# Two decode attention blocks on one core: the last four heads of an output projection in 2 KB rows, and the first output stored ahead

## The chip, the cores and the metric

The kernel runs on one core of one Trainium2 chip. The metric is the device time of one execution in microseconds (us), lower is better. Before the change the median of three runs is 665.49 us (665.38 to 665.52).

## The reference

Two independent attention blocks, A and B, of the same sizes, each for a single query token against a cache of 8192 positions and 32 heads of 128. Their outputs of 512 numbers stand side by side in the result.

```python
def _A_ref(x, k_cache, v_cache, wq, wo):          # _B_ref computes the same (rep is 1)
    B, Sq, D = x.shape                             # 1, 1, 512
    H, Dh = 32, 128
    q = (x @ wq).reshape(B, Sq, H, Dh).transpose(0, 2, 1, 3)
    scores = jnp.einsum("bhqd,bhkd->bhqk", q, k_cache) * (Dh ** -0.5)
    p = _softmax(scores, axis=-1)
    o = jnp.einsum("bhqk,bhkd->bhqd", p, v_cache)
    return o.transpose(0, 2, 1, 3).reshape(B, Sq, H * Dh) @ wo     # wo: 4096 x 512
...
return jnp.concatenate([a, b], axis=-1)            # (1, 1, 1024), bf16
```

## The kernel before

**Loops and groups.** The work is 16 groups of four heads: eight groups of A, then eight of B. A group's K and V are 8 MB each; K goes to one of two slots of `kn`, V to the only slot `vn`. In each of the 16 rounds VectorE multiplies K by the query (L279), TensorE sums over the head dimension with identity matmuls into the two tiles of `rps` (L424, L430), VectorE reduces them to scores `s_sb` (L307), ScalarE takes exponentials (L379), and TensorE multiplies by V into `acc` (L483). One round later VectorE turns `acc` into the group's four output columns: `part()` (L284, L287, L291), a small matmul `total_of_group()` (L436), and `outs()` (L296).

**The order of transfers.** One queue, SyncE's, issues nearly everything in the order in which it is written: K and V by turns, then `wo` of A (4 MB), the last V, and `wo` of B in the six pieces of the table `WOB` (L89): heads 0 to 15, 16 to 23, 24 to 27, 28 and 29, 30, 31. The flag in the table says how a piece lies in memory. With True, partition p takes n consecutive rows of `wo` of the n heads, one run of n KB. With False, partition p takes row p of each head, runs of 1 KB.

**What the layout costs.** With the runs of n KB, a head's output vector no longer fits the rows that its `wo` tile holds, so the outputs of these heads are redistributed first: `spread(i)` (VectorE, L328) writes them into `zb` under a mask, a matmul with `jsel` (L449) moves them into PSUM, and `lay(i)` (VectorE, L336) copies them to `o2`. This is done for A (32 heads) and for the three long pieces of B in the last round, in `mid()` on TensorE and after the loop on VectorE. The last four heads, whose outputs come last, are written to `o2` directly (L347).

**The end of the program.** On TensorE, after the last matmuls with V: 16 matmuls with the first piece of B (`partial`, L443) into `yps[0]`, which also holds A's sum over its 32 heads; five matmuls whose result nobody reads (`turn_over(5)`, L461); `total_of_group()` for the last four heads; four fp32 passes with `sel16` (L496) that add up the rows of `yps[0]` into `yps[1]`, after ScalarE has copied them to `yc` (L382; `yc` is a view of `qmem` and shows under that name); and 32 matmuls for B's heads 16 to 31 (L505), each half of a head's 512 columns, a row for A and a row for B each. Before each piece of `wo` TensorE waits for its semaphore. Then ScalarE and VectorE each cast half of the columns to `out_sb` (L384, L349), and SyncE stores both outputs with one DMA of two 1 KB rows (L232).

Of the kernel before, what the change touches and what calls it, by code (L numbers as in the profile page):

```python
# [8 lines left out]
BF16 = mybir.dt.bfloat16  # L9
F32 = mybir.dt.float32  # L10

P = 128
# [33 lines left out]
def bass_concat_heads__mha_block_cached__gqa_block_cached__decode_kernel(  # L46
# [26 lines left out]
    G = 4  # L73
    HP = P // G
# [3 lines left out]
    N = NA * GA  # L78
# [7 lines left out]
    NG = T // W  # L86


    WOB = [(0, 16, True), (16, 8, True), (24, 4, True), (28, 2, False), (30, 1, False), (31, 1, False)]  # L89
    RG = [32, 16, 8, 4]  # L90
    NH = NOUT // 2

    with ExitStack() as st:
# [11 lines left out]
        WO = H * NOUT  # L105
# [3 lines left out]
        yc = qmem[:, 0:NOUT]  # L109
# [21 lines left out]
        o2 = sb("o2", [P, NA * H, NA], BF16)  # L131
        mask = {g: sb("mask%d" % g, [P, P // g], BF16) for g in RG}
        jsel = {g: sb("jsel%d" % g, [P, g], BF16) for g in RG}
        out_sb = sb("out_sb", [NA, NOUT], BF16)

        def ps(name, shape):
            return ec(nc.psum_tensor(name, shape, F32))
# [2 lines left out]
        acc = ps("acc", [P, 512])  # L140
# [2 lines left out]
        misc = ps("misc", [P, 512])  # L143
        yps = [ps("yps%d" % i, [P, 512]) for i in range(2)]
        EX = 128
        lay_ps = [misc, yps[1], acc, mtp]

        def sem(name):
            return ec(nc.semaphore(name))
# [3 lines left out]
        s_wob = [sem("s_wob%d" % g) for g in range(len(WOB))]  # L153
        s_k = [sem("s_k%d" % i) for i in range(2)]

        c_pool, c_sel, c_mul, c_sr, c_g, c_gm, c_self, c_st, c_o, c_rl, c_yd = (
            sem(n) for n in ("c_pool", "c_sel", "c_mul", "c_sr", "c_g", "c_gm", "c_self", "c_st", "c_o", "c_rl", "c_yd"))

        c_qa, c_nb, c_p, c_ya = (sem(n) for n in ("c_qa", "c_nb", "c_p", "c_ya"))

# [25 lines left out]
        @block.sync  # L186
        def _(e):
            load_wq(e, 0)
            for a in range(NA):
                e.dma_start(xrow[a:a + 1, :], xs[a][0]).then_inc(s_x, 16)  # L190

            def group(x, n):
                a, i = divmod(n, GA)
                return x[a][0, G * i:G * (i + 1)].rearrange("h (p t) d -> (h p) (t d)", p=HP)

            def load_k(n):
                if n >= 2:
                    e.wait_ge(c_red, RED * (n - 1))
                e.dma_start(kn[:, n % 2 * KS:(n % 2 + 1) * KS], group(ks, n)).then_inc(s_k[n % 2], 16)

            def load_v(n):
                if n:
                    e.wait_ge(c_pv, n + 1)
                else:
                    e.wait_ge(c_q, N)
                e.dma_start(vn[:], group(vs, n)).then_inc(s_v, 16)

            def load_wob(g):
                h0, n, rows = WOB[g]
                src = wos[1][h0 * Dh:(h0 + n) * Dh, :]  # L210
                dst = kn[:, WO + h0 * NOUT:WO + (h0 + n) * NOUT]
                if rows:
                    src = src.rearrange("(p j) n -> p (j n)", p=P)
                elif n > 1:
                    src = src.rearrange("(j p) n -> p j n", p=P)
                    dst = dst.rearrange("p (j n) -> p j n", j=n)
                e.dma_start(dst, src).then_inc(s_wob[g], 16)

            load_k(0)
            load_k(1)  # L220
            for n in range(N - 1):
                load_v(n)
                if n + 2 < N:
                    load_k(n + 2)
            e.wait_ge(c_red, RED * (N - 1))
            e.dma_start(kn[:, 0:WO], wos[0].rearrange("(p j) n -> p (j n)", p=P)).then_inc(s_woa, 16)
            load_v(N - 1)
            for g in range(len(WOB)):
                load_wob(g)
            e.wait_ge(c_yd, 1)  # L230
            e.wait_ge(c_ya, 2)
            e.dma_start(out[0].rearrange("o (a n) -> (o a) n", a=NA), out_sb[:]).then_inc(s_out, 16)  # L232
            e.wait_ge(s_out, 16)

        def once(e):

# [6 lines left out]
        def _(e):  # L243
            with once(e):
# [48 lines left out]
                def outs(dst):  # L293
                    w_self()
                    w_ex()
                    e.tensor_tensor(dst, mtp[:, EX:EX + G], rinv[:], ALU.mult).then_inc(c_o, 1)  # L296
# [20 lines left out]
                        outs(oD[:, bass.ds(r * G, G)])  # L317


                todo = [(0, 0, H)] + [(1, h0, n) for h0, n, rows in WOB if rows]  # L320
                e.wait_ge(c_o, N)

                def spread(i):
# [15 lines left out]

                spread(0)  # L340
                spread(1)
                for i in range(len(todo)):
                    lay(i)
                    if i + 2 < len(todo):
                        spread(i + 2)
                part()
                outs(o2[:, NA * H - G:NA * H, NA - 1])  # L347
                e.wait_ge(c_y, 2)
                e.tensor_copy(out_sb[:, 0:NH], yps[1][0:NA, 0:NH]).then_inc(c_yd, 1)  # L349


        @block.scalar
        def _(e):
            load_wq(e, 1)
            with once(e):
                w_q = _Stepped(e, c_q, 1, 1)
                w_bc = _Stepped(e, c_bc, 1, 1)
                w_nb = _Stepped(e, c_nb, 1, 1)
                w_pv = _Stepped(e, c_pv, 1, 1)
                e.wait_ge(c_pv, 1)  # L360
                e.copy(xT[:].rearrange("p (a c) -> p c a", c=C),
                       misc[:, 0:C * NA].rearrange("p (c a) -> p c a", a=NA)).then_inc(c_qa, 2)
                with e.Fori(0, N // 2) as r:
                    for j in range(2):
                        w_q()
                        for h in range(G):
                            p = slice(h * HP, (h + 1) * HP)
                            i = e.copy(qflat[p, bass.ds(r * (2 * Dh) + j * Dh, Dh)],  # L368
                                       yps[j][p, h * Dh:(h + 1) * Dh])
                        i.then_inc(c_qa, 1)  # L370
                e.wait_ge(c_pool, NPOOL)
                with e.Fori(0, N):
                    w_bc()
                    e.activation(negb[:], bmp[:, 0:G], AF.Copy, scale=-scale).then_inc(c_nb, 1)  # L374
# [7 lines left out]
                e.copy(yc, yps[0][:]).then_inc(c_ya, 1)  # L382
                e.wait_ge(c_y, 2)
                e.copy(out_sb[:, NH:NOUT], yps[1][HP:HP + NA, 0:NH]).then_inc(c_ya, 1)  # L384


        @block.tensor
        def _(e):
            with once(e):
# [51 lines left out]
                def partial(h):  # L441
                    k = h % G * HP
                    return e.matmul(yps[0][k:k + NA, :], o2[:, h, :], wo_rows(h), start=False, stop=False,  # L443
                                    skip_group_check=True)

                def mid():
                    for i, (a, h0, n) in enumerate([(0, 0, H)] + [(1, h0, n) for h0, n, rows in WOB if rows]):
                        e.wait_ge(c_rl, (1, 2, 4, 6)[i])
                        e.matmul(lay_ps[i][:, 0:n], zb[:, i % 2, :], jsel[n][:], start=True,  # L449
                                 stop=True).then_inc(c_rm, 1)  # L450
                    e.matmul(yps[0][:], zrow[:], ones_bf[0:1, 0:1].broadcast_to([1, 512]), start=True,
                             stop=False, skip_group_check=True)
                    e.wait_ge(c_rl, 8)
                    e.wait_ge(s_woa, 16)
                    for h in range(H):
                        partial(h)

                def turn_over(n):

                    with e.Fori(0, n):  # L460
                        e.matmul(rps[:, 0, :], ident[:], kn[:, 0:512], start=True, stop=True)  # L461
# [27 lines left out]
                for h in range(H, H + WOB[0][1]):  # L489
                    m = partial(h)  # L490
                m.then_inc(c_y, 1)
                turn_over(5)
                total_of_group()
                e.wait_ge(c_ya, 1)
                for b in range(2):
                    e.matmul(yps[1][b * HP:b * HP + NA, 0:NH], sel16[:, 0, 0:NA],  # L496
                             yc[:, b * NH:(b + 1) * NH], start=True, stop=False, skip_group_check=True)
                for g in range(1, len(WOB)):
                    h0, n, rows = WOB[g]
                    e.wait_ge(s_wob[g], 16)  # L500
                    for h in range(h0, h0 + n):
                        for b in range(2):
                            if h == H - G - 1 and b:
                                e.wait_ge(c_o, N + 1)
                            m = e.matmul(yps[1][b * HP:b * HP + NA, 0:NH], o2[:, H + h, :],  # L505
                                         wo_rows(H + h)[:, b * NH:(b + 1) * NH], start=False,
                                         stop=(h == H - 1), skip_group_check=True)
                m.then_inc(c_y, 1)
# [28 lines left out]
```

## Time and profile before

| what | value |
|---|---|
| median of 3 runs | 665.49 us (665.38 to 665.52) |
| profiled execution: its span, first to last instruction | 663.5 us |
| PE, DVE, ACT busy | 58%, 55%, 12% of the span |
| DMA engines | nine tenths busy or more in nearly every slice, 430 GB/s mean |
| mean granted TensorE clock | 0.79 |

The profiled execution has no time of its own beside its span; 2.0 us lie between the span and the median. PE is TensorE's matmul, PEld its weight load, DVE is VectorE, ACT ScalarE, SP SyncE; a number after L is a line of the kernel. In the views by time the first column is the start in us from the span's start, the second the duration. A matmul's duration includes its pipeline, so a stream of matmuls is read by the distance of their starts. The tile names leave the buffer's number out: `yps` is `yps[0]` or `yps[1]`, `o` is `o2`, `sel` is `sel16`, `m` is `m1`.

### The profile page before, as it was taken

Reading aid. Unit: us, or ns where it says so; the run is one execution under the profiler, and the core shown is the slowest. Engines: PE = TensorE matmul, PEld = TensorE weight load, DVE = VectorE, ACT = ScalarE, POOL = GpSimd, SP = SyncE. Lnnn points to the kernel's source line nnn. Section 1 sums busy time; section 2 is a strip of 40 time slices with the busy share of each in tenths; the row PEclk is TensorE's granted clock in tenths of the full one; section 3 lists DMA queues with packets and bytes.
Section 4 is the critical chain, followed back from the end, with each engine's and each line's share of the span. In section 5 each row is a group of like instructions: output and inputs, shape, how many; then the busy total and the mean of one; then the engine's idle time right before and its main releaser. Section 6 shows DMA issues by size and latency. Waiting matters only on the chain.

```text
span 663.5 us, 7942 instructions
## 1 busy us (share of the span) xinstructions
PE 385.8 (58%) x2402; PEld 191.8 (29%) x2402; DVE 362.5 (55%) x249; ACT 76.6 (12%) x212; POOL 2.3 (0%) x12
## 2 busy tenths in 40 slices
PE   0455685854819185481918548191854819185488
PEld 0122232423315042330404233140423314032233
DVE  1009494848292754829274482927548292744821
ACT  0370202020010202001020200102020010202002
POOL 1000000000000000000000000000000000000000
PEclk9995988786959678695967869596786959678697
DMA  9999998999999999999999999999999999999997
GB/s 379 443 442 442 442 442 379 442 442 442 442 442 442 391 431 442 442 442 442 442 399 423 442 442 442 442 442 411 411 442 442 442 442 442 415 407 442 440 444 317
DMA packets 6041, 285.23 MB, mean 430 GB/s; under 512 B 660, under 2 KB 1176, under 8 KB 1304
## 3 DMA queue, kind: packets, MB, share of 16 engines
q1 hardware_dynamic: 5896, 281.03, 98.0%
q10 hardware_dynamic: 144, 4.19, 1.5%
q14 instruction: 1, 0.01, 0.0%
HBM read 285.21 MB, written 0.00 MB: 430 GB/s over the span
## 4 chain that ended last, share of the span: by engine, by line
DMA 72%; PE 22%; DVE 2%; issue 2%; ACT 1%; ACTq 0%; DVEq 0%; SPq 0%
DMA vn<-in_B_v_cache_dram 34%; DMA vn<-in_A_v_cache_dram 34%; PE acc L483 14%; PE rps L430 5%; DMA xrow<-in_B_x_dram 3%; PE yps L413 2%; DVE kn L279 1%; ACT qmem L368 1%; PE yps L443 1%; ACT pt L379 0%; PE yps L505 0%; DVE s_sb L307 0%; PE rps L461 0%; PE misc L478 0%; PE rps L424 0%
## 5 line engine op out<-in xcount | busy, mean ns | idle before, releaser
L279 DVE TENSOR_TENSOR kn<-kn,qmem 128x16384 bf16<-128x16384 bf16 x32 | 276.7, 8688 | 55.2 <-ACT qmem L368 43.0
L430 PE MATMUL rps<-kn,ident 128*128 x1024 | 236.8, 383 | 0.4
L483 PE MATMUL acc<-vn,pt 128*32 128x512 bf16 x1024 | 92.3, 531 | 145.7 <-DMA vn<-in_B_v_cache_dram 75.3
L307 DVE TENSOR_REDUCE s_sb<-rps 128x64 f32<-128x512 f32 x64 | 44.1, 691 | 165.1 <-PE rps L430 165.1
L430 PEld LDWEIGHTS rps<-kn,ident 128*128 128x128 bf16 x1024 | 96.4, 98 | 111.0 <-issue 22.6
L483 PEld LDWEIGHTS acc<-vn,pt 128*32 128x32 bf16 x1024 | 60.3, 127 | 171.1 <-issue 155.9
L374 ACT ACTIVATE negb<-bmp 128x4 f32<-128x4 f32 x16 | 2.8, 173 | 539.7 <-PE bmp L472 539.7
L379 ACT ACTIVATE pt<-s_sb,negb 32x256 bf16<-32x256 f32 x64 | 54.9, 858 | 4.3 <-ACT negb L374 2.9
L478 PE MATMUL misc<-rsum,ones_f 128*128 128x4 f32 x32 | 9.4, 365 | 56.4 <-ACT pt L379 56.4
L284 DVE TENSOR_SCALAR om<-acc,msk 128x128 f32<-128x128 f32 x16 | 5.6, 350 | 42.8 <-PE acc L483 42.8
L478 PEld LDWEIGHTS misc<-rsum,ones_f 128*128 128x128 f32 x32 | 8.0, 312 | 58.6 <-ACT pt L379 57.8
L413 PE MATMUL yps<-vn,xT 128*128 x64 | 17.3, 419 | 6.2 <-ACT qmem L368 4.2
L287 DVE SCALAR_TENSOR_TENSOR om<-acc,msk,om 128x128 f32<-128x128 f32 x48 | 16.8, 351 | 5.9
L470 PE MATMUL mtp<-ident_f,m 128*1 128x128 f32 x32 | 6.1, 270 | 22.6 <-DVE m L312 22.6
L424 PE MATMUL rps<-ones_bf,zrow 1*128 1x1 bf16 x64 | 11.0, 171 | 13.4 <-DVE kn L279 10.8
L424 PEld LDWEIGHTS rps<-ones_bf,zrow 1*128 1x128 bf16 x64 | 5.8, 91 | 40.6 <-issue 40.6
L368 ACT CAST qmem<-yps 32x128 f32 x64 | 16.4, 256 | 7.0 <-PE yps L413 6.3
L379 ACT ACTIVATION_READ_ACCUMULATOR pt<-s_sb,negb 32x1 f32 x64 | 15.9, 249 | 0.0
L399 PE MATMUL misc<-ident,xrow 2*128 2x2 bf16 x4 | 0.3, 166 | 22.8 <-DMA xrow<-in_B_x_dram 22.8
L413 PEld LDWEIGHTS yps<-vn,xT 128*128 x64 | 6.6, 103 | 16.5 <-issue 13.7
L472 PE MATMUL bmp<-gm,ones_f 1*128 1x4 f32 x32 | 6.1, 258 | 7.3 <-DVE gm L314 7.3
L470 PEld LDWEIGHTS mtp<-ident_f,m 128*1 128x1 f32 x32 | 1.4, 80 | 30.5 <-DVE m L312 30.5
(58 smaller groups left out, 57.0 us busy)
## 6 DMA issues: line engine op xcount, KB each, us to landing
vn<-in_B_wq_dram ACTq DMA_DIRECT2D x1, 4096.0 KB, 21.9
vn<-in_A_wq_dram SPq DMA_DIRECT2D x1, 4096.0 KB, 21.7
kn<-in_A_wo_dram SPq DMA_DIRECT2D x1, 4096.0 KB, 27.4
kn<-in_B_wo_dram SPq DMA_DIRECT2D x1, 2048.0 KB, 27.7
kn<-in_B_wo_dram SPq DMA_DIRECT2D x1, 1024.0 KB, 29.7
kn<-in_B_wo_dram SPq DMA_DIRECT2D x1, 512.0 KB, 30.5
kn<-in_B_wo_dram SPq DMA_DIRECT2D x1, 256.0 KB, 30.8
kn<-in_B_wo_dram SPq DMA_DIRECT2D x2, 128.0 KB, 30.6
```

Of the source, the lines that this page charges most:

```text
L279: e.tensor_tensor(k, k, qflat[:, bass.ds(q, Dh)].unsqueeze(1).broadcast_to([P, HM, Dh]), ALU.mult).then_inc(c_mul, 2)
L287: e.scalar_tensor_tensor(om[t % 2][:], acc[:, t * Dh:(t + 1) * Dh], msk[:, t:t + 1], om[(t + 1) % 2][:], ALU.mult, ALU.add).then_inc(*((c_ ...
L307: e.tensor_reduce(s_sb[:, h * HT:(h + 1) * HT], rps[:, h % 2, :].rearrange("p (t d) -> p t d", d=DW), AX.X, ALU.add).then_inc(c_sr, 1)
L368: i = e.copy(qflat[p, bass.ds(r * (2 * Dh) + j * Dh, Dh)], yps[j][p, h * Dh:(h + 1) * Dh])
L379: e.activation(pt[p, 0:T, h], s_sb[p, :], AF.Exp, bias=negb[p, h:h + 1], scale=scale, accum_out=rsum[p, h:h + 1]).then_inc(c_p, 4)
L413: i = e.matmul(yps[j][:], xT[:, bass.ds(x0 + c, 1)].broadcast_to([P, P]), vn[:, bass.ds(w0 + (c * H * Dh + j * G * Dh), G * Dh)], start=(c ...
L424: e.matmul(rps[:, tile, 0:1], zrow[:], ones_bf[0:1, 0:1], start=True, stop=False, skip_group_check=True)
L430: m = e.matmul(ro, ident[:], src, start=False, stop=False, skip_group_check=True)
L443: return e.matmul(yps[0][k:k + NA, :], o2[:, h, :], wo_rows(h), start=False, stop=False, skip_group_check=True)
L470: e.matmul(mtp[0:1, 0:P], m1[:], ident_f[:], start=True, stop=True).then_inc(c_gx, 1)
L478: e.matmul(misc[:, 0:G], ones_f[:], rsum[:], start=True, stop=True)
L483: m = e.matmul(acc[k:k + HP, :], ptf[:, g * W * G:g * W * G + HP], vn[:, g * W * Dh:(g + 1) * W * Dh], start=(g < G), stop=(g >= NG - G))
```

## The change

The table's last two pieces become one, so that B's last four heads arrive in two pieces of two heads. Both take the layout that the longer pieces have (over the four heads together), in runs of 2 KB a partition. The outputs of these heads therefore go through `spread` and `lay` too, into the free PSUM tile `bmp`. A's output row is finished ahead: the passes with `sel16` stand before `total_of_group()`, give A's sum in `rps[:, 1, :]` and B's in `yps[1]`, and are twice as many; the matmuls for B's heads 16 to 31 have one row instead of two. `turn_over` runs twice instead of five times. ScalarE casts each output in one copy of 33 partitions (partitions 0 and 32 hold the two halves of the columns), VectorE casts nothing, and SyncE stores each output as two rows of 512 bytes.

```diff
-    WOB = [..., (24, 4, True), (28, 2, False), (30, 1, False), (31, 1, False)]
+    WOB = [..., (24, 4, True), (28, 2, False), (30, 2, False)]
...
-        out_sb = sb("out_sb", [NA, NOUT], BF16)
+        out_sb = sb("out_sb", [HP + 1, NA * NH], BF16)
...
-        lay_ps = [misc, yps[1], acc, mtp]
+        lay_ps = [misc, yps[1], acc, mtp, bmp]
...  # SyncE, load_wob
                 if rows:
-                    src = src.rearrange("(p j) n -> p (j n)", p=P)
-                elif n > 1:
-                    src = src.rearrange("(j p) n -> p j n", p=P)
-                    dst = dst.rearrange("p (j n) -> p j n", j=n)
-                e.dma_start(dst, src).then_inc(s_wob[g], 16)
+                    src = wos[1][h0 * Dh:(h0 + n) * Dh, :].rearrange("(p j) n -> p (j n)", p=P)
+                else:
+                    j0 = h0 - (H - G)
+                    src = wos[1][(H - G) * Dh:H * Dh, :].rearrange("(p j) n -> p (j n)", p=P)[
+                        :, j0 * NOUT:(j0 + n) * NOUT]
+                e.dma_start(kn[:, WO + h0 * NOUT:WO + (h0 + n) * NOUT], src).then_inc(s_wob[g], 16)
...  # SyncE, the end
-            e.wait_ge(c_yd, 1)
-            e.wait_ge(c_ya, 2)
-            e.dma_start(out[0].rearrange("o (a n) -> (o a) n", a=NA), out_sb[:]).then_inc(s_out, 16)
-            e.wait_ge(s_out, 16)
+            for a in range(NA):
+                e.wait_ge(c_ya, 2 + a)
+                e.dma_start(out[0, :, a * NOUT:(a + 1) * NOUT].rearrange("o (b n) -> (o b) n", b=2),
+                            out_sb[0:HP + 1:HP, a * NH:(a + 1) * NH]).then_inc(s_out, 16)
+            e.wait_ge(s_out, 32)
...  # VectorE, the end
-                outs(o2[:, NA * H - G:NA * H, NA - 1])
-                e.wait_ge(c_y, 2)
-                e.tensor_copy(out_sb[:, 0:NH], yps[1][0:NA, 0:NH]).then_inc(c_yd, 1)
+                outs(oD[:, N * G:N * G + G])
+                e.wait_ge(c_o, N + 1)
+                spread(last)
+                lay(last)
...  # ScalarE, the end
-                e.wait_ge(c_y, 2)
-                e.copy(out_sb[:, NH:NOUT], yps[1][HP:HP + NA, 0:NH]).then_inc(c_ya, 1)
+                for a, t in enumerate((rps[:, 1, :], yps[1][:])):
+                    e.wait_ge(c_y, 2 + a)
+                    e.copy(out_sb[:, a * NH:(a + 1) * NH], t[0:HP + 1, 0:NH]).then_inc(c_ya, 1)
...  # TensorE, the end
-                turn_over(5)
+                turn_over(2)
+                e.wait_ge(c_ya, 1)
+                for a, t in ((1, yps[1][:]), (0, rps[:, 1, :])):
+                    for b in range(2):
+                        m = e.matmul(t[b * HP:b * HP + 1, 0:NH], sel16[:, 0, a:a + 1],
+                                     yc[:, b * NH:(b + 1) * NH], start=True, stop=(a == 0),
+                                     skip_group_check=True)
+                m.then_inc(c_y, 1)
                 total_of_group()
-                e.wait_ge(c_ya, 1)
-                for b in range(2):
-                    e.matmul(yps[1][b * HP:b * HP + NA, 0:NH], sel16[:, 0, 0:NA],
-                             yc[:, b * NH:(b + 1) * NH], start=True, stop=False, skip_group_check=True)
                 for g in range(1, len(WOB)):
                     h0, n, rows = WOB[g]
+                    if g == 2:
+                        layout(len(ns) - 1)
+                    if g == 3:
+                        e.wait_ge(c_rl, 10)
                     e.wait_ge(s_wob[g], 16)
                     for h in range(h0, h0 + n):
                         for b in range(2):
-                            if h == H - G - 1 and b:
-                                e.wait_ge(c_o, N + 1)
-                            m = e.matmul(yps[1][b * HP:b * HP + NA, 0:NH], o2[:, H + h, :],
+                            m = e.matmul(yps[1][b * HP:b * HP + 1, 0:NH], o2[:, H + h, 1:2],
                                          wo_rows(H + h)[:, b * NH:(b + 1) * NH], start=False,
                                          stop=(h == H - 1), skip_group_check=True)
```

On TensorE, from the end of `turn_over` on, the instructions stood before as follows; `s_wob1` is the semaphore of the second piece of `wo` of B, and so on, `c_ya` ScalarE's, `c_st` and `c_o` VectorE's.

```order
L436 MATMUL mtp<-selh,om 128x4 [waits c_st]
L496 MATMUL yps<-qmem,sel 2x256 [waits c_ya]
L496 MATMUL yps<-qmem,sel 2x256
L505 MATMUL yps<-kn,o 2x256 [waits s_wob1]
L505 MATMUL yps<-kn,o 2x256 x15
L505 MATMUL yps<-kn,o 2x256 [waits s_wob2]
L505 MATMUL yps<-kn,o 2x256 x6
L505 MATMUL yps<-kn,o 2x256 [waits c_o]
L505 MATMUL yps<-kn,o 2x256 [waits s_wob3]
L505 MATMUL yps<-kn,o 2x256 x3
L505 MATMUL yps<-kn,o 2x256 [waits s_wob4]
L505 MATMUL yps<-kn,o 2x256
```

After the change the same stretch of TensorE reads as follows; the lines of the program are a few numbers higher, so that L439 is the former L436, L454 the former L449, L505 the former L496 and L519 the former L505, and `c_rl` is the semaphore of `spread` and `lay`.

```order
L505 MATMUL yps<-qmem,sel 1x256 [waits c_ya]
L505 MATMUL yps<-qmem,sel 1x256
L505 MATMUL rps<-qmem,sel 1x256 x2
L439 MATMUL mtp<-selh,om 128x4 [waits c_st]
L519 MATMUL yps<-kn,o 1x256 [waits s_wob1]
L519 MATMUL yps<-kn,o 1x256 x15
L454 MATMUL bmp<-jsel,zb 128x4 [waits c_rl]
L519 MATMUL yps<-kn,o 1x256 [waits s_wob2]
L519 MATMUL yps<-kn,o 1x256 x7
L519 MATMUL yps<-kn,o 1x256 [waits s_wob3,c_rl]
L519 MATMUL yps<-kn,o 1x256 x3
L519 MATMUL yps<-kn,o 1x256 [waits s_wob4]
```

The passes with `sel`, and with them the wait for ScalarE's copy, now stand ahead of the small matmul of `total_of_group()`; a matmul of the layout stands between the second and the third piece; and the last wait is for a piece of two heads (three more matmuls follow it). On VectorE the end of the program changes as follows (of before and of the change in one piece).

```order
-L296 TENSOR_TENSOR o<-mtp,rinv 128x4 [waits c_ex,c_self]
-L349 CAST out_sb<-yps 2x256 [waits c_y]
+L296 TENSOR_TENSOR oD<-mtp,rinv 128x4 [waits c_ex,c_self]
+L329 TENSOR_TENSOR zb<-oD,mask 128x128 [waits c_rm,c_o]
+L337 CAST o<-bmp 128x4 [waits c_rm]
```

The cast of the output is gone from VectorE, and the two steps of the layout stand behind the last four output columns.

More of the change, by code (lines that the diff above doesn't have):

```diff
@@ L86, in bass_concat_heads__mha_block_cached__gqa_block_cached__decode_kernel @@
     NG = T // W
-    WOB = [(0, 16, True), (16, 8, True), (24, 4, True), (28, 2, False), (30, 1, False), (31, 1, False)]
+    WOB = [(0, 16, True), (16, 8, True), (24, 4, True), (28, 2, False), (30, 2, False)]
     RG = [32, 16, 8, 4]
@@ L154, in bass_concat_heads__mha_block_cached__gqa_block_cached__decode_kernel @@
         s_k = [sem("s_k%d" % i) for i in range(2)]
-        c_pool, c_sel, c_mul, c_sr, c_g, c_gm, c_self, c_st, c_o, c_rl, c_yd = (
-            sem(n) for n in ("c_pool", "c_sel", "c_mul", "c_sr", "c_g", "c_gm", "c_self", "c_st", "c_o", "c_rl", "c_yd"))
+        c_pool, c_sel, c_mul, c_sr, c_g, c_gm, c_self, c_st, c_o, c_rl = (
+            sem(n) for n in ("c_pool", "c_sel", "c_mul", "c_sr", "c_g", "c_gm", "c_self", "c_st", "c_o", "c_rl"))
         c_qa, c_nb, c_p, c_ya = (sem(n) for n in ("c_qa", "c_nb", "c_p", "c_ya"))
@@ L209, in load_wob @@
                 h0, n, rows = WOB[g]
-                src = wos[1][h0 * Dh:(h0 + n) * Dh, :]
-                dst = kn[:, WO + h0 * NOUT:WO + (h0 + n) * NOUT]
                 if rows:
-                    src = src.rearrange("(p j) n -> p (j n)", p=P)
-                elif n > 1:
-                    src = src.rearrange("(j p) n -> p j n", p=P)
-                    dst = dst.rearrange("p (j n) -> p j n", j=n)
-                e.dma_start(dst, src).then_inc(s_wob[g], 16)
+                    src = wos[1][h0 * Dh:(h0 + n) * Dh, :].rearrange("(p j) n -> p (j n)", p=P)
[4 more added lines that the diff above has]
+                e.dma_start(kn[:, WO + h0 * NOUT:WO + (h0 + n) * NOUT], src).then_inc(s_wob[g], 16)
             load_k(0)
@@ L317, in _ @@
                         outs(oD[:, bass.ds(r * G, G)])
-                todo = [(0, 0, H)] + [(1, h0, n) for h0, n, rows in WOB if rows]
+                todo = [(0, 0, H)] + [(1, h0, n) for h0, n, rows in WOB if rows] + [(1, H - G, G)]
+                last = len(todo) - 1
                 e.wait_ge(c_o, N)
@@ L341, in _ @@
                 spread(1)
-                for i in range(len(todo)):
+                for i in range(last):
                     lay(i)
-                    if i + 2 < len(todo):
+                    if i + 2 < last:
                         spread(i + 2)
                 part()
-                outs(o2[:, NA * H - G:NA * H, NA - 1])
-                e.wait_ge(c_y, 2)
-                e.tensor_copy(out_sb[:, 0:NH], yps[1][0:NA, 0:NH]).then_inc(c_yd, 1)
+                outs(oD[:, N * G:N * G + G])
+                e.wait_ge(c_o, N + 1)
+                spread(last)
+                lay(last)
         @block.scalar
@@ L444, in partial, with layout @@
                                     skip_group_check=True)
+                ns = [H] + [n for h0, n, rows in WOB if rows] + [G]
+                def layout(i):
+                    n = ns[i]
+                    e.wait_ge(c_rl, (1, 2, 4, 6, 9)[i])
+                    e.matmul(lay_ps[i][:, 0:n], zb[:, i % 2, :], jsel[n][:], start=True,
+                             stop=True).then_inc(c_rm, 1)
                 def mid():
[L447 to L450, printed above, removed]
+                    for i in range(len(ns) - 1):
+                        layout(i)
                     e.matmul(yps[0][:], zrow[:], ones_bf[0:1, 0:1].broadcast_to([1, 512]), start=True,
```

## The prediction

> **What bounds the kernel now.** I read the page first, then the chain of waits, then the timeline of the last microseconds.
>
> ```profile
> DMA 72%; PE 22%; DVE 2%; issue 2%; ACT 1%; ACTq 0%; DVEq 0%; SPq 0%
> HBM read 285.21 MB, written 0.00 MB: 430 GB/s over the span
> ```
>
> Transfers carry the chain, and every byte read before is still read after, in the same order; nothing ahead of the last V is touched. Only the tail can change. This is the end of the chain (start, duration, what):
>
> ```profile
> 656.87 0.86 PE yps L443 x11
> 657.73 1.19 PE rps L461 x5
> 658.92 0.23 PE mtp L436 x2
> 659.15 0.53 PE yps L496 x4
> 659.68 1.90 PE yps L505 x30
> 661.61 0.29 PE yps L505 x2
> 661.92 0.41 DVE out_sb L349
> ```
>
> The chain names TensorE for the last five microseconds, but the timeline shows what TensorE waited for in them:
>
> ```profile
> 657.41 1.30 DVE L287 SCALAR_TENSOR_TENSOR om<-acc,msk,om 128x128 f32<-128x128 f32 x3
> 657.79 0.58 ACT L382 COPY qmem<-yps 128x512 f32<-128x512 f32 x1 [7.97 <-PE yps L443]
> 658.76 0.38 PE L436 MATMUL mtp<-selh,om 128*128 128x4 f32 x2
> 659.08 0.60 PE L496 MATMUL yps<-qmem,sel 128*2 128x256 f32 x4
> 659.25 0.16 DVE L296 TENSOR_TENSOR o<-mtp,rinv 128x4 bf16<-128x4 f32 x1 [0.46 <-PE mtp L436]
> 659.29 1.40 PEld L505 LDWEIGHTS yps<-kn,o 128*2 128x2 bf16 x24
> 659.51 2.37 PE L505 MATMUL yps<-kn,o 128*2 128x256 bf16 x32
> 660.94 0.09 PEld L505 LDWEIGHTS yps<-kn,o 128*2 128x2 bf16 x4 [0.25 <-DMA kn<-in_B_wo_dram]
> 661.31 0.08 PEld L505 LDWEIGHTS yps<-kn,o 128*2 128x2 bf16 x2 [0.28 <-DMA kn<-in_B_wo_dram]
> 661.60 0.08 PEld L505 LDWEIGHTS yps<-kn,o 128*2 128x2 bf16 x2 [0.21 <-DMA kn<-in_B_wo_dram]
> 661.92 0.36 ACT L384 CAST out_sb<-yps 2x256 bf16<-2x256 f32 x1 [3.55 <-PE yps L505]
> 661.92 0.41 DVE L349 CAST out_sb<-yps 2x256 bf16<-2x256 f32 x1 [2.50 <-PE yps L505]
> 662.37 0.27 SPq L232 DMA_DIRECT2D out_dram<-out_sb  x1
> ```
>
> The last three pieces of `wo` of B each end a wait of 0.21 to 0.28 us. So the end is: the last piece visible at 661.60, its two matmuls and the hand-over until 661.92, VectorE's cast until 662.33, the store from 662.37 to the span's end at 663.5. TensorE had at most a quarter of a microsecond to spare before each piece. The question is whether the pieces come earlier, and whether TensorE, which gets more to do, is still ready for them.
>
> **The change part by part.** *The pieces in 2 KB runs.* Three stretches of the trace (duration, then busy time by engine, granted clock, DMA share, GB/s) lie within pieces of one run length: 8 KB (heads 16 to 23), 4 KB (24 to 27), 1 KB (28 to 31).
>
> ```profile
> 656.00:658.00 2.00, 2.00 (x37) 0.77 (x27) 0.82 (x3) 0.21 (x1) 0.00 (x0) 1.00 0.99 414
> 658.20:659.20 1.00, 1.00 (x8) 0.49 (x8) 0.47 (x3) 0.17 (x1) 0.00 (x0) 1.00 0.99 401
> 659.80:660.70 0.90, 0.90 (x20) 0.75 (x18) 0.00 (x0) 0.00 (x0) 0.00 (x0) 1.00 1.11 359
> ```
>
> The four heads are 524,288 bytes: 1.46 us at 359 GB/s, 1.31 us at 401. Runs of 2 KB lie between; I take the middle, 380 GB/s, 1.38 us, so the last piece comes 0.08 us earlier, with bounds of 0 (the rate stays) and 0.15 (that of 4 KB runs). It is visible at 661.52. [...]
>
> *TensorE before the pieces.* Three idle matmuls go, but the passes with `sel` move ahead of the last group's small matmul and wait for ScalarE's copy. That copy starts when the 16 matmuls of L443 are done, which does not change, and ends at 657.79 + 0.58 = 658.37; the two remaining idle matmuls (five took 1.19 from 657.73) are over by 658.2. A hand-over of 0.05 (VectorE's `om` ends at 658.71, TensorE starts at 658.76) lets the passes start at 658.42. Four of them took from 659.08 to the next start at 659.51, 0.43; eight take 0.86, until 659.28. Queued behind them are the small matmul, ready since 658.76, and all who wait for it: it is 0.52 late. From its start to the next took 0.32, so the 16 matmuls with heads 16 to 23 start at 659.60, only 0.09 later than before. At the pace of the 24 weight loads that ran in 1.40 (0.058 each; one column instead of two changes nothing, since the 256 streamed columns set the pace), they end at 660.53.
>
> *The layout.* How long its steps take shows where the last round does them for the other heads:
>
> ```profile
> 646.28 0.16 DVE L296 TENSOR_TENSOR oD<-mtp,rinv 128x4 f32 x1 [0.91 <-PE mtp L436]
> 646.52 0.49 DVE L328 TENSOR_TENSOR zb<-oD,mask 128x128 bf16<-128x128 bf16 x2
> 646.88 0.19 PE L449 MATMUL misc<-jsel,zb 128*128 128x32 bf16 x1 [0.75 <-DVE zb L328]
> 647.07 0.18 PE L449 MATMUL yps<-jsel,zb 128*128 128x16 bf16 x1
> 647.10 0.20 DVE L336 CAST o<-misc 128x32 bf16<-128x32 f32 x1
> ```
>
> The small matmul at 659.28 gives the outputs a start at 659.77 (0.49 later, as 658.76 to 659.25), `spread` at 660.01 (+0.24), the layout's matmul not before 660.37 (+0.36). TensorE comes to it at 660.53, so it does not wait. It holds TensorE for at most 0.19, until 660.72. The cast starts at 660.75 (+0.22), ends by 660.95 and is seen at 661.00. Meanwhile TensorE does heads 24 to 27, eight matmuls of 0.058, until 661.18: the layout is covered, by 0.18 us. If that cover were gone, each further 0.1 us would be paid in full from 0.3 us on. Heads 28 and 29 (loaded by about 660.85) last until 661.41. TensorE waits for the last piece at 661.52, with 0.11 to spare where it had 0.21.
>
> *From the last piece to the end.* Two heads follow the last wait instead of one: two more matmuls, which run in pairs, add 2 x 0.058 = 0.12. The hand-over to ScalarE is then at 661.92 - 0.08 + 0.12 = 661.96. ScalarE's cast takes 0.36 (33 partitions instead of 2, the same 256 columns), while VectorE's 0.41 was the later one before: 0.05 less. The store starts at 662.37 - 0.08 + 0.12 - 0.05 = 662.36. The wait at its end is this row:
>
> ```profile
> SPq L233 <- DMA out_dram<-out_sb: 0.9, 1, 0.9
> ```
>
> It stays: half the bytes in each of two rows; I take 0.02 off, between 0 and 0.1.
>
> *A's store ahead.* Its passes end at about 659.4, ScalarE casts until 659.9, SyncE has nothing else to issue and sends 1 KB. It queues behind pieces already issued and lands before the last store, more than two microseconds later. What covers it is the whole end of B, so it costs nothing; uncovered it would cost the 0.27 of an issue.
>
> **Sum.** -0.08 + 0.12 - 0.05 - 0.02 = -0.03 us: the span becomes 663.5, the time 665.46, if the 2.0 us around the span stay. [...] With the bounds (-0.15 to 0 for the pieces, -0.1 to 0 for the store, 0 to +0.12 for the second pair, since some of it may fit before the last piece is complete) the sum lies between -0.3 and +0.1. What the change saves in transfer it spends on having more work behind the last wait. A measurement of this kernel can tell about 0.2%, 1.3 us, from no change, so I forecast no change.
>
> **Rivals.** *The clock falls (slower).* `turn_over` goes from five to two, and it fills the time in which the granted clock is decided. The trace shows that it is decided in stretches of 3.41 us (duration, PE busy, ..., granted clock):
>
> ```profile
> 56.68:60.09 3.41, 2.67 (x7) 1.06 (x8) 3.41 (x2) 0.00 (x0) 0.00 (x0) 0.50 0.71 308
> 60.09:63.50 3.41, 3.41 (x9) 1.21 (x8) 3.41 (x1) 0.00 (x0) 0.00 (x0) 0.50 1.42 615
> 94.23:97.64 3.41, 1.54 (x8) 0.49 (x5) 3.03 (x7) 0.00 (x0) 0.00 (x0) 1.00 1.42 615
> 97.64:101.05 3.41, 2.64 (x12) 1.25 (x13) 1.06 (x2) 0.00 (x0) 0.00 (x0) 1.00 0.71 308
> 449.21:452.63 3.42, 1.19 (x7) 0.68 (x6) 1.55 (x4) 0.37 (x2) 0.00 (x0) 1.00 1.42 613
> 452.63:456.04 3.41, 0.03 (x1) 0.03 (x1) 2.56 (x1) 3.24 (x8) 0.00 (x0) 0.50 0.71 308
> 650.60:654.01 3.41, 3.41 (x34) 1.36 (x30) 0.00 (x0) 0.00 (x0) 0.00 (x0) 0.50 1.07 456
> 654.01:657.42 3.41, 3.41 (x68) 1.47 (x60) 0.36 (x2) 0.00 (x0) 0.00 (x0) 1.00 0.93 392
> 657.43:660.84 3.41, 3.41 (x43) 1.90 (x35) 1.28 (x5) 0.58 (x1) 0.00 (x0) 1.00 1.01 376
> ```
>
> At full clock 1.54 us of work in a stretch kept it, 1.19 lost it. After the change the last stretch is idle for about 0.25 us (658.2 to 658.42) and so keeps it, unless the matmuls of one column do not count as work. Then only the two idle matmuls, 2 x 0.24 us, of the stretch count, and from its end on TensorE runs at half pace. With the end at 660.84 as here, heads 24 to 27, 28 to 31 and the last latency cost about 0.4 more, 665.9; with an end at 659.5, everything behind it, about 1.5 more, 667.0; from an end at 659.7 or earlier on it passes the 1.3 us. Against it: the stretch 650.60:654.01 won the clock back with matmuls of two columns in its first 1.4 us, though 2.67 us of full matmuls did not suffice at 56.68. Chance 8%, 3% of it over the bound. [...]
>
> *The layout comes onto the path.* Six hand-overs stand between ScalarE's copy and heads 28 to 31. If each is 0.05 longer, and the passes, now into two PSUM tiles, take 0.2 longer, the 0.5 us meet 0.11 us to spare before the last piece, and some 0.4 are paid: 665.8. For it: every spare time above is below 0.2. Against: all steps are taken from rows of the same shapes. Chance 15%.
>
> *The shorter end pays.* If 2 KB runs reach the pace of 4 KB ones, the second pair hides, and the store of halves is 0.1 shorter, the time is 665.2. Chance 15%.
>
> [...]
>
> **How the numbers follow.** The forecast, 665.46, holds 60% (665.3 to 665.6); the layout 15%, the shorter end 15%, the clock 8%, anything unseen 2%. The range takes in the first three with 0.1 for the level of a run, and the clock at this trace's phase: 665.1 to 666.0. Faster by over 0.2% means under 664.16, a whole 1.3 us out of a tail whose transfers end at 661.1 anyway: 2%. Slower by over 0.2% is above 666.82: 3% for the clock, 2% for a wait unseen, 5%. Within: 93%.
>
> **What would show it.** Right: three waits for pieces of `wo` become two, the last ending near 661.5 after the same start of the last V; the passes with `sel` start 0.05 after ScalarE's copy; the layout's matmul has no wait of its own; one cast of 0.36 ends the chain. Wrong: a granted clock of 0.5 before 662; TensorE waiting for `zb` or for `o`; the last weight loads released by VectorE, not by a DMA; the early store's issue or landing in the last wait of SyncE.

## The result and the profile after

The changed kernel takes 669.5 us (669.4 to 670.17, five runs) where the kernel before took 665.38 in the same comparison: ratio 1.0062, 95% interval 1.0051 to 1.0073. Slower by 4.1 us; no change had been forecast.

The span of the page and the three pieces that end the chain, of the changed kernel:

```profile
span 665.0 us, 7943 instructions
630.18 31.37 DMA kn<-in_B_wo_dram
661.60 0.40 PE yps L519 x4
662.02 0.36 ACT out_sb L387
```

The span is 1.5 us longer than the 663.5 of before, in a kernel that is 4.1 us slower. So there are two losses: one in the span, and a larger one behind it, where no instruction of the kernel stands. The chain ends in the last piece of `wo`, the last matmuls and one cast, as the prediction has it. The tail's timeline:

```profile
657.60 0.59 ACT L384 COPY qmem<-yps 128x512 f32<-128x512 f32 x1 [7.90 <-PE yps L446]
658.24 0.60 PE L505 MATMUL yps<-qmem,sel 128*1 128x256 f32 x4 [0.15 <-ACT qmem L384]
659.20 0.39 PE L439 MATMUL mtp<-selh,om 128*128 128x4 f32 x2
659.52 1.04 PE L519 MATMUL yps<-kn,o 128*1 128x256 bf16 x16
660.48 0.10 PEld L454 LDWEIGHTS bmp<-jsel,zb 128*128 128x128 bf16 x1 [0.22 <-issue]
661.59 0.09 PEld L519 LDWEIGHTS yps<-kn,o 128*1 128x1 bf16 x4 [0.45 <-DMA kn<-in_B_wo_dram]
662.02 0.36 ACT L387 CAST out_sb<-yps 33x256 bf16<-33x256 f32 x1 [2.33 <-PE yps L519]
662.41 0.48 SPq L231 DMA_DIRECT2D out_dram<-out_sb  x1
SPq L233 <- DMA out_dram<-out_sb: 2.1, 1, 2.1
```

Until the last store is issued, at 662.41 against 662.37, nothing is lost. Then the issue takes 0.48 instead of 0.27, and SyncE waits 2.1 us for the store instead of 0.9: nearly all of the span's 1.5 us. What lies in the DMA engines then is seen when the queues are asked in short stretches. First before, from 663.0 to 663.5 and from 663.5 to 664.1; then after, from 663.5 to 663.6, 663.7 to 664.0, 664.0 to 664.2 and 666.0 to 668.5 (each pair: packets in the stretch, and their queue):

```profile
DMA packets 4, 0.00 MB, mean 4 GB/s; under 512 B 2, under 2 KB 4, under 8 KB 4
q1 hardware_dynamic: 4, 0.00, 1.5%
...
DMA packets 1, 0.01 MB, mean 14 GB/s; under 512 B 0, under 2 KB 0, under 8 KB 0
q14 instruction: 1, 0.01, 5.1%
```

```profile
DMA packets 2, 0.00 MB, mean 5 GB/s; under 512 B 1, under 2 KB 2, under 8 KB 2
q1 hardware_dynamic: 2, 0.00, 2.4%
...
DMA packets 1, 0.01 MB, mean 27 GB/s; under 512 B 0, under 2 KB 0, under 8 KB 0
q14 instruction: 1, 0.01, 6.4%
...
DMA packets 2, 0.00 MB, mean 3 GB/s; under 512 B 1, under 2 KB 2, under 8 KB 2
q1 hardware_dynamic: 2, 0.00, 1.1%
...
DMA packets 1, 0.02 MB, mean 7 GB/s; under 512 B 0, under 2 KB 0, under 8 KB 0
q8 instruction: 1, 0.02, 3.2%
```

Queue 1 carries the kernel's data: a packet for each row of the store, and one of 4 bytes as the row ends (at 663.16 and 663.20 before). Before, both rows go out together, and an 8 KB packet on queue 14, which the view lists as instructions, follows them. After, one row goes out in the first stretch, then the instruction packet, and the second row only behind it. The trace has the packets' times to 0.01 us: here, and in three of the runs below (`e2_code_down`, `e3_store_apart`, `e4_two_short`), the second row starts in the moment in which the instruction packet ends (664.10 here). That both pass through one DMA engine is my reading of these times; the trace does not name the engine. And at 666.9, two microseconds after the span's end, there is a packet that the kernel before does not have: 16 KB of instructions on queue 8. The last semaphore events of the trace come at 670.1, 5.1 us behind the span; before they came 1.4 behind it. The execution does wait for this packet: the semaphore events pause at 665.8, the packet has landed at 668.2, and they go on at 669.7, where the pause of before is 0.2 us long. In the four runs below that also have the late packet the events go on 1.4 to 1.6 us after it has landed, too.

Two theories follow. **Store**: the store's shape (two rows of 512 bytes, 32 partitions apart, or there being two stores) delays the rows until they meet the instruction packet. **Code**: TensorE's compiled program has grown from 477 instructions to 488 (two more fp32 matmuls of four instructions each, the layout's matmul, a wait), and one more packet of instructions is fetched at its end, the 16 KB on queue 8. Each theory has the other as its rival: that it explains the whole loss.

### The profile page after: what moved, and what is told of

It is laid out like the page before. It is cut to its first block, busy times and chain, and to the rows that moved or that the text cites. A ratio compares the mean times of both kernels' runs of the same rounds, so it can differ in the third digit from the quotient of the medians.

```text
span 665.0 us, 7943 instructions
## 1 busy us (share of the span) xinstructions
PE 385.4 (58%) x2404; PEld 191.3 (29%) x2404; DVE 362.6 (55%) x250; ACT 77.0 (12%) x213; POOL 2.3 (0%) x12
## 4 chain that ended last, share of the span: by engine, by line
DMA 76%; PE 18%; DVE 2%; issue 1%; ACT 1%; SPq 0%; ACTq 0%; DVEq 0%
DMA vn<-in_B_v_cache_dram 34%; DMA vn<-in_A_v_cache_dram 34%; PE acc L492 13%; DMA kn<-in_B_wo_dram 5%; DMA xrow<-in_B_x_dram 3%; PE rps L433 3%; PE yps L416 2%; DVE kn L279 1%; ACT qmem L370 1%; ACT pt L381 0%; SPq L216 0%; ACTq L43 0%; ACTq L370 0%; DVE s_sb L307 0%; PE misc L487 0%
## 5 line engine op out<-in xcount | busy, mean ns | idle before, releaser
L296 DVE TENSOR_TENSOR oD<-mtp,rinv 128x4 f32 (+1 forms) x16 | 2.6, 163 | 15.0 <-PE mtp L439 15.0
```

## The experiments

In these runs the kernel before has a median of 665.07 to 665.13 us, with a median span of 663.7 to 663.9 and 1.3 us between span and time, so the time of each run is split in the same way, into its span and what lies outside it.

**More code behind the kernel's work (`e1_code_up`).** The kernel before, with:

```diff
                 m.then_inc(c_y, 1)
+                for i in range(6):
+                    e.matmul(rps[:, 0, 0:1], zrow[:], ones_bf[0:1, 0:1], start=True, stop=True)
```

> The kernel before, with six tiny matmuls (a column each) put behind the last matmul of TensorE's program: 12 more instructions, 489 instead of 477 (the changed kernel has 488), run while the output is cast and stored. Theory code (the growth of TensorE's program makes one more fetch of instructions necessary after the last store, and the end of the execution waits for it): span 663.5 as before, a 16 KB instruction packet some 3 us after the span, time 668.1 (+2.7). Rival store (all of the loss comes from the new stores, the time outside the span included): time 665.4.

Measured: 668.89 us, ratio 1.0054 (1.0037 to 1.0071). The median span is 663.9, and 4.8 us lie outside it instead of 1.3. The late packet is there (from 665.5 to 667.5):

```profile
DMA packets 1, 0.02 MB, mean 8 GB/s; under 512 B 0, under 2 KB 0, under 8 KB 0
q8 instruction: 1, 0.02, 2.9%
```

The loss outside the span needs neither the new stores nor anything else of the change.

**Less code in the changed kernel (`e2_code_down`).**

```diff
-                    for h in range(H):
+                    for h in range(H - 6):
                         partial(h)
```

> The changed kernel with the matmuls of A's heads 26 to 31 left out of its output projection: 12 instructions less on TensorE, 476. Theory code: no 16 KB packet at the end, 2.0 us instead of 4.7 outside the span, the span still 664.8 to 665.0, time 666.8. Rival store: span and time as in the changed kernel, 669.5. A mixed cause elsewhere in the change (the early store, the order of the passes) would also leave 669.5.

Measured: 666.31 us, ratio 1.0020 (1.0010 to 1.0030). Median span 665.0, outside 1.3: the code's part is gone, the store's part stays. The price outside was larger than expected (3.4 instead of 2.7), so the time fell half a microsecond further. One thing was not as expected: a 16 KB packet on queue 8 is still there (from 663.3 to 664.4):

```profile
q8 instruction: 1, 0.02, 5.3%
```

It starts at 663.6, 2.3 us ahead of that execution's span end at 665.9, and the time outside the span is not longer for it.

**The same store from partitions apart (`e3_store_apart`).** The kernel before, its rows 32 partitions apart:

```diff
...  # out_sb gets 33 partitions, set to zero at the start
-            e.dma_start(out[0].rearrange("o (a n) -> (o a) n", a=NA), out_sb[:]).then_inc(s_out, 16)
+            e.dma_start(out[0].rearrange("o (a n) -> (o a) n", a=NA), out_sb[0:HP + 1:HP, :]).then_inc(s_out, 16)
```

> The kernel before, whose one store takes its two 1 KB rows from partitions 0 and 32 instead of 0 and 1 (the row from partition 32 is zeros, so B's output is left out; one memset more at the start). Theory apart (rows from partitions 32 apart are given to the DMA engines one after the other): the second row about 0.6 us behind the first, SyncE's wait at the end 2.1 instead of 0.9, span 664.6 to 665.0, time 666.6 to 666.9. Rival short (rows of 512 bytes are what costs) and rival two (two stores cost): span 663.5, time 665.4.

Measured: 666.48 us, ratio 1.0022 (1.0013 to 1.0032), median span 665.0. The issue, the wait, and the packets from 663.55 to 664.1 and from 664.1 to 664.3:

```profile
662.47 0.58 SPq L233 DMA_DIRECT2D out_dram<-out_sb  x1
SPq L234 <- DMA out_dram<-out_sb: 1.8, 1, 1.8
...
DMA packets 3, 0.01 MB, mean 17 GB/s; under 512 B 1, under 2 KB 2, under 8 KB 2
q14 instruction: 1, 0.01, 6.1%
q1 hardware_dynamic: 2, 0.00, 0.7%
...
DMA packets 2, 0.00 MB, mean 5 GB/s; under 512 B 1, under 2 KB 2, under 8 KB 2
q1 hardware_dynamic: 2, 0.00, 1.7%
```

Rows of 1 KB from partitions apart cost what the changed kernel's rows of 512 bytes cost: the issue takes 0.58, and again the second row goes out only behind the instruction packet. One store is enough for that, and so are long rows.

**Two stores of short rows from adjacent partitions (`e4_two_short`).**

```diff
-            e.dma_start(out[0].rearrange("o (a n) -> (o a) n", a=NA), out_sb[:]).then_inc(s_out, 16)
-            e.wait_ge(s_out, 16)
+            for j in range(2):
+                e.dma_start(out[0].rearrange("o (a n) -> (o a) n", a=NA)[:, j * NH:(j + 1) * NH],
+                            out_sb[:, j * NH:(j + 1) * NH]).then_inc(s_out, 16)
+            e.wait_ge(s_out, 32)
```

> The kernel before, whose output is stored by two DMAs of two 512-byte rows from partitions 0 and 1, both at the end. Theory apart: each store costs what the one of 1 KB rows did, the second is issued 0.27 to 0.3 us after the first, span 663.8, time 665.7. Rival short: the wait at the end is 2.1 or more, span 664.8 to 665.3, time 666.8 to 667.3. Rival two: the second store alone adds over 1 us, the same.

Measured: 666.30 us, ratio 1.0021 (1.0011 to 1.0032), median span 665.0. My expectation for this run was wrong by 0.6 us. By the span alone both rivals, short rows and two stores, came nearer (665.0 against 664.8 to 665.3); the trace shows what happened:

```profile
662.48 0.59 SPq L233 DMA_DIRECT2D out_dram<-out_sb  x2
SPq L235 <- DMA out_dram<-out_sb: 1.8, 1, 1.8
```

Each issue takes the usual 0.27 (0.59 for both and the gap between them), so short rows are not slow to issue. But the second store comes 0.3 later, its second row starts behind the instruction packet (at 664.10, when the packet has left), and the wait is as long as in the run before. So the last row need not lie in a partition apart to be late: here 0.3 us of delay from a second issue is enough. Whether a delay of any other cause does the same was not tried.

**ScalarE ends later (`e5_late_act`).** The store from partitions apart once more, and in ScalarE's program, as its last step:

```diff
+                e.wait_ge(s_out, 16)
```

> The store from partitions 0 and 32 again (two rows of 1 KB, the row from partition 32 is zeros), and ScalarE does not end its program before the store has landed. In the run without this wait an 8 KB packet of instructions, which starts 1.4 us after ScalarE's program ends, stood ahead of the second row on its DMA engine. Theory collision: with ScalarE ending later that packet comes after the store, the two rows start within 0.1 us of each other again, SyncE's wait at the end falls from 1.8 to 1.0 to 1.3 us, span 664.1 to 664.4. Rival slow rows (rows from partitions 32 apart go out one after the other by themselves): the second row stays 0.4 us or more behind, the wait 1.8, span 664.9. For the time neither promises a gain, since the end of ScalarE's program then comes later: 666.0 to 666.6.

Measured: the wait, and the packets from 663.8 to 664.0 and from 665.5 to 666.5:

```profile
SPq L234 <- DMA out_dram<-out_sb: 1.0, 1, 1.0
...
DMA packets 4, 0.00 MB, mean 10 GB/s; under 512 B 2, under 2 KB 4, under 8 KB 4
q1 hardware_dynamic: 4, 0.00, 3.7%
...
DMA packets 1, 0.01 MB, mean 8 GB/s; under 512 B 0, under 2 KB 0, under 8 KB 0
q14 instruction: 1, 0.01, 2.9%
```

With ScalarE ending after the store, the instruction packet comes at 665.8 instead of 663.6, both rows go out together again, and the wait falls from 1.8 to 1.0. So the theory of the run `e3_store_apart`, that rows from partitions apart go out one after the other, does not hold; the collision made the second one late. Median span 664.4; the time, 666.68 (ratio 1.0021, 1.0011 to 1.0031), does not fall, since ScalarE's later end is paid outside the span (2.3 us).

**Code size by itself (`e6_code_start`, `e7_code_half`, `e11_code_486`).** The kernel before with six, three or five tiny matmuls where TensorE waits for data at the start:

```diff
                 e.wait_ge(c_pool, NPOOL)
+                for i in range(6):      # 3, 5
+                    e.matmul(rps[:, 0, 0:1], zrow[:], ones_bf[0:1, 0:1], start=True, stop=True)
                 e.wait_ge(s_x, 32)
```

> The kernel before with six tiny matmuls (one column) at the start of TensorE's program, where it waits for data for 20 us: 488 instructions, as many as the changed kernel. Theory code size (where TensorE's program ends against a block of instructions decides whether the end needs a late fetch): a 16 KB instruction packet 1.4 to 2 us after the span, time 668.3 to 668.9, span 663.6 to 664.0. Rival late matmuls (the matmuls at the end themselves kept TensorE from ending in time): time as before, 665.1.

> As the kernel with six tiny matmuls at the start, with three of them: 482 instructions, between the 477 of before and the 488 of the changed kernel. Theory code size says only that there is an edge between 477 and 488: either no late packet and 665.1, or the packet and 668.3 to 668.9; nothing between (rival gradual: each instruction costs its part, 666.9).

> The kernel before with five tiny matmuls at the start of TensorE's program: 486 instructions, to close in on the edge between 482 and 488. Code size: either the late packet and 668.3 to 668.9, or none and 665.1.

| TensorE's instructions | time, us | median span | outside | ratio (95%) |
|---|---|---|---|---|
| 482 | 665.28 | 663.8 | 1.6 | 1.0002 (0.9993 to 1.0012) |
| 486 | 668.65 | 663.9 | 4.8 | 1.0052 (1.0033 to 1.0071) |
| 488 | 668.33 | 663.7 | 4.7 | 1.0046 (1.0029 to 1.0062) |

The added matmuls run in the first 20 us, beside a wait for data, and the whole price appears at the end. It is a step between 482 and 486, not a slope. (486 has two executions, 488 four, 482 ten.) Whether the instructions stand at the end of the program, as in `e1_code_up`, or at its start makes no difference to the price (4.8 us outside the span there, 4.7 here with 488). The packet of the run with 488 (from 665 to 667) is the changed kernel's:

```profile
DMA packets 1, 0.02 MB, mean 8 GB/s; under 512 B 0, under 2 KB 0, under 8 KB 0
q8 instruction: 1, 0.02, 3.0%
```

So the step cost 3.4 us here (4.7 us outside the span with 488 instructions, 1.3 in the kernel before). What sets the place of the step was not shown.

**The stores mended alone (`e10_store_mended`).** In the changed kernel each output becomes one row of 1 KB on partition 0, by one more cast each:

```diff
-                    e.copy(out_sb[:, a * NH:(a + 1) * NH], t[0:HP + 1, 0:NH]).then_inc(c_ya, 1)
+                    for b in range(2):
+                        e.copy(out_sb[:, a * NOUT + b * NH:a * NOUT + (b + 1) * NH],
+                               t[b * HP:b * HP + 1, 0:NH]).then_inc(c_ya, 1)
```

> The changed kernel with one thing mended, the stores: each output is one row of 1 KB from partition 0 (ScalarE casts each half by itself, so one cast of 0.36 us more lies ahead of B's store); TensorE keeps its 488 instructions. Two losses that add: SyncE's wait at the end 0.9, span 664.0 to 664.2 (the second cast in it), the 16 KB packet still 1.4 to 2 us after the span, time 668.5 to 669.0. Rival one cause (the late packet comes from the late store): no late packet, 665.5.

Measured: 668.9 us, ratio 1.0050 (1.0035 to 1.0066), the wait 0.9 again, median span 664.3 (with the further cast in it), outside 4.6, the late packet there. The two losses add; neither is a consequence of the other. The change's two stores are both still there, so the wait does not come from their number. Of the six executions one took 666.04 us, with only 1.8 outside the span: the late fetch is not paid in every execution, and the runs do not show why. All other executions of the kernels with the late packet, the changed one included, have 3.8 us or more outside.

**Both mended (`e8_both_mended`).** As one row each, cast by ScalarE and VectorE side by side for B, and TensorE's program cut to 475 instructions:

```diff
-                turn_over(2)
                 e.wait_ge(c_ya, 1)
-                for a, t in ((1, yps[1][:]), (0, rps[:, 1, :])):
...
+                for b in range(2):
+                    e.matmul(yps[1][b * HP:b * HP + 1, 0:NH], sel16[:, 0, 1:2],
+                             yc[:, b * NH:(b + 1) * NH], start=True, stop=False, skip_group_check=True)
+                e.matmul(rps[0:1, 1, :], sel16[:, 0, 0:1], yc[:], start=True, stop=True).then_inc(c_y, 1)
```

> The changed kernel with both suspected losses taken out: each output is stored as one row of 1 KB from partition 0 (A cast in one copy of 512 columns, B's halves by VectorE and ScalarE side by side), and TensorE's program is cut to 475 instructions (one matmul for A's sum, no idle matmuls, two waits put on instructions that had none). Theory of two losses (store 1.1, code 3.4): no late packet that is waited for, SyncE's wait at the end 0.9, span 663.6 to 663.9, time 665.0 to 665.3, that of the kernel before. Rival third loss (something else of the change costs too): above 665.6.

Measured: 665.34 us, ratio 1.0000 (0.9991 to 1.0010), median span 664.0, outside 1.3.

```profile
662.77 0.26 SPq L233 DMA_DIRECT2D out_dram<-out_sb  x1
SPq L235 <- DMA out_dram<-out_sb: 0.9, 1, 0.9
```

With both gone the change is worth nothing, as forecast. For this version, whose TensorE program also differs at the end, a third loss above 0.1% is excluded.

**The rows alone (`e9_rows_alone`).** The kernel before with only the two pieces of 2 KB runs and their layout:

```diff
-    WOB = [..., (28, 2, False), (30, 1, False), (31, 1, False)]
+    WOB = [..., (28, 2, False), (30, 2, False)]
...
-                outs(o2[:, NA * H - G:NA * H, NA - 1])
+                outs(oD[:, N * G:N * G + G])
+                e.wait_ge(c_o, N + 1)
+                spread(last)
+                lay(last)
...
```

> One part of the change alone: the last four heads in two pieces of 2 KB runs with the layout, everything else (both outputs in every matmul, five idle matmuls, two casts, one store of two 1 KB rows from partitions 0 and 1) as before; TensorE's program has 479 instructions, below the 482 that ended without a late packet. Step of the prediction on the pieces: the last piece 0.08 us earlier (0 to 0.15), two more matmuls behind it 0.12, so 0.0 to +0.1 us: time 665.1, span 663.6 to 663.8, the layout's matmul without a wait of its own. Rival layout on the path: the last matmuls released by VectorE, 0.3 to 0.5 us more.

Measured: 664.99 us, ratio 0.9997 (0.9988 to 1.0007), median span 663.7. The layout's matmul and the last weight loads:

```profile
660.98 0.10 PEld L454 LDWEIGHTS bmp<-jsel,zb 128*128 128x128 bf16 x1 [0.23 <-issue]
661.96 0.09 PEld L516 LDWEIGHTS yps<-kn,o 128*2 128x2 bf16 x4 [0.34 <-DMA kn<-in_B_wo_dram]
```

The layout is covered, and the last piece is what is waited for. None of the runs is faster than the kernel before by more than the uncertainty.

## Why the prediction was wrong

**Right: everything up to the last store's issue.** The passes with `sel` start 0.05 after ScalarE's copy (658.19 to 658.24) and take 0.96 until the small matmul instead of 0.86. Heads 16 to 23 start at 659.52 (659.60 forecast), and their 16 matmuls of one column take 1.04 us, as those of two columns do in `e9_rows_alone`; the layout's matmul waits for no `zb`, one cast of 0.36 ends the chain, and the store is issued at 662.41 (662.36). TensorE even waits 0.45 us for the last piece, where 0.11 had been left. The runs of 2 KB come at the rate that was taken for them (380 GB/s):

```profile
659.90:660.60 0.70, 0.70 (x15) 0.39 (x11) 0.29 (x1) 0.00 (x0) 0.00 (x0) 1.00 1.02 378
```

From the end of the last 4 KB run to the end of the last run of `wo` it is 1.34 us instead of 1.45, also in the run `e9_rows_alone`. But in this execution the 4 KB runs end 0.11 later than before (659.76 against 659.65), so the last piece is visible at 661.59, not 661.52, and the 0.08 does not appear in the time. The clock rival did not occur; with two idle matmuls and matmuls of one column the clock stays (duration, PE busy, ..., granted clock):

```profile
656.55:659.97 3.42, 3.27 (x38) 1.30 (x40) 1.62 (x7) 0.95 (x2) 0.00 (x0) 1.00 0.99 400
659.97:663.38 3.41, 1.86 (x29) 0.81 (x23) 0.38 (x2) 0.36 (x1) 0.00 (x0) 1.00 0.25 92
```

**Wrong: "It stays: half the bytes in each of two rows; I take 0.02 off, between 0 and 0.1."** I priced the store by its bytes and allowed no loss. It measured +0.2 in the issue and +1.2 in the wait. The rows' distance of 32 partitions costs 0.4 to 0.5 us: the first row goes out 1.12 us after the issue's start, and 1.22 with rows of 1 KB, where it was 0.74 before. With the collision taken away (`e5_late_act`) the median span is still 0.7 over before. This delay is enough to bring the second row behind the end's instruction packet, which costs the rest. In the median spans of the changed kernel: 664.8 against 663.7.

**Wrong: "if the 2.0 us around the span stay."** That was carried as a condition and never priced. It is the larger term: 4.7 us outside the span instead of 1.3, and a longer TensorE program is enough for it. The 2.0 itself set the span of one execution against the median of others; where both are recorded for the same executions it is 1.3. The profile of before could not show how near the edge was, but that the end fetches instructions was in it: the page's one packet on queue 14 lies at the very end, at 663.5. The prediction should have listed the program's growth (11 instructions) among the things that the change adds, with a rival that ends on the slower side outside the span; it had left 2% for a wait unseen.

**Not tested by itself:** that A's store ahead costs nothing holds as far as the runs go, since with both losses mended the early store remains and the time is that of before.

**What stays open.** Why the changed kernel with 476 instructions still fetches a 16 KB packet, only earlier (at 663.6), while the kernels with 475, 477, 479 and 482 show none, was not settled; so the count of instructions does not by itself say which kernels fetch it. Nor was it tried which other lengths of TensorE's program have such an edge. Nor is the cause of the extra wait behind the instruction packet shown: the last event on the store's semaphore comes 0.81 us after the second row's packet of 4 bytes ends (664.94 against 664.13), where it was 0.31 before (663.52 against 663.20). The run with ScalarE's later end, in which the whole delay is gone, does not separate it from the row's late start.

## What to carry to other kernels

The end of this program cost 1.1 us more in the span and 3.4 more behind it, and no term of the kernel named either. Compare the span with the time, and ask the DMA queues for packets behind the last store, before calling a change of the tail free. Count an engine's instructions when code is added, since a step at an unknown edge cost 3.4 us here. Store the last rows with one store from adjacent partitions, or as one row: the wait was 0.9 us that way, and 1.8 to 2.1 where the instruction packet came ahead of the last row.

## What was not expected of the hardware

- A store whose two rows lie 32 partitions apart holds SyncE's issue for 0.48 to 0.59 us instead of 0.27.
- An 8 KB packet of instructions starts 0.9 to 1.5 us after ScalarE's last copy (1.2 in `e3_store_apart`, where the expectation of `e5_late_act` says 1.4), and later when ScalarE ends later. A last row that is not out by then went out only when it had passed (it takes 0.3 to 0.5 us), and the store was complete 0.8 us later than without it (wait 1.8 against 1.0).
- With 482 instructions in TensorE's program the execution ends 1.6 us after the span, with 486 it ends 4.8 us after it.
